# Four output accumulators per batch, a short lag between the two products, and the first batch's attention in quarters

## The chip, the cores and the metric

The kernel runs on one core of one Trainium2 chip. The metric is the device time of one execution in microseconds (us); less is better. TensorE is called PE below, VectorE DVE, ScalarE ACT, GpSimd POOL and SyncE SP. PE's results go to PSUM tiles; the kernel's two pools of them hold eight buffers of 128 x 512 fp32 between them.

## The reference

There are 8 batches and 8 heads, with x of 512 rows and state of 32 rows per head, 64 wide. State and x attend to one another, and the result, 8 x 544 rows of 512, goes through a two-layer network of width 2048.

```python
scores = scale * x @ state.T          # per batch and head, 512 x 32
xread = softmax(scores) @ state       # 512 x 64
scores2 = scale * state @ x.T         # 32 x 512
sread = softmax(scores2) @ x          # 32 x 64
y = concat([xread, sread], axis=2)    # 544 x 64, then heads side by side: 544 x 512
h = y @ w_in                          # 4352 x 2048
out = gelu_exact(h) @ w_out           # 4352 x 512, fp32
```

## The kernel before

**The work of a batch.** xread is never formed. `pmat` multiplies state by w_in into a tile P (256 x 2048 per batch, the two halves of the heads as two tiles of 128 rows), so that the first product is AT x P. `rearr` arranges x in the layout `x4`, `xtr` transposes it on PE into PSUM and DVE copies it out as `xT`; `scores` multiplies it by the block-diagonal state `sbd` into a PSUM tile pt, and ACT takes the exponential into `e`; `norm` (on DVE) sums over the 32 state rows, inverts and multiplies into `a`; `atr` transposes `a` to AT. `sread` (two halves, t = 0 and 1) multiplies `e` by `x4`, DVE scales the result into `srm`, and `srt` transposes that into XSR, where the state rows of all batches are collected.

**The two products.** `mm1(b, m)` makes chunk m (of 16) of the hidden layer for the 512 rows of batch b: two matmuls of 128 x 512 into a PSUM tile hp, then a gelu on ACT into `g`. `mm2` adds four chunks of `g` times w_out to one of four groups of 128 output rows: four matmuls into an accumulator `op`; four such quarters finish a group, DVE copies it to `osb`, and SP sends it out. `mm1_sr` and `mm2_sr` do the same for the 256 collected state rows at the end.

**The buffers.** `ps_f` has six buffers and holds everything short-lived: hp, the P tiles (two per 512 columns), transposes, pt, sread's and srt's results. `ps_o` has two, for the output accumulators. An accumulator's four quarters follow one another, so one or two groups are open at a time.

**The order.** It is written out by hand (`manual_schedule`): each engine runs its instructions in the order of the calls. A step is one `mm1` and, once 16 steps are done (`lag = 16`), one `mm2` call; the dictionaries `extra` (batches 0 and 1) and `steady` (the rest) put the attention of the next batch and the P groups between the steps. In `steady`, step 0 and 1 hold xtr, step 3 scores and norm, step 7 two P groups together, step 9 atr, steps 11 and 12 sread, step 13 two more P groups, step 14 srt. So a batch's output products run 16 steps behind its first products.

**The start.** The four quarters of batch 0's x (two heads each) are loaded as fp32, two by SP's queue and two by ACT's, and cast and arranged by DVE (`rearr0`); PE transposes them (`xtr0`), ACT copies all four out. `keep_warm` issues matmuls on a zero tile, 20 in all before the first product. All weights and the other batches' x are cast to bf16 by DMAs of the POOL queue, in the order w_in 0 and 1, the state, x1, w_in 2 and 3, w_out 0 and 1, x2, w_out 2 and 3, x3. At most eight of these transfers are under way: the ninth waits for the first to land.

The softmax here doesn't subtract the row's maximum and nothing guards it: scores larger than these inputs give would overflow.

## Time and profile before

| what | value |
| --- | --- |
| runs | 243.44, 243.13, 241.72 us (median 243.13) |
| the profiled execution, its own time | 240.81 us |
| its span in the profile | 238.6 us |
| granted TensorE clock, mean | 0.998 |
| PE busy | 223.9 us (94%) |
| ACT busy / DVE busy / POOL busy | 124.9 (52%) / 104.8 (44%) / 28.4 us (12%) |
| DMA busy share, first 48 us | about 0.8 to full, then about 0.1 to 0.4 |
| first mm1 starts | 14.73 us |
| first mm2 starts | 31.91 us |
| batch 2, 3 and 4 begin (first transposes in step 0) | 61.86, 86.73, 111.61 us |
| last matmul's copy begins / end of span | 234.85 / 238.6 us |

The profile is one execution, recorded by the hardware. The span is the time from the first to the last instruction in it; the execution's own time is 2.2 us longer. A line of a group or of the timeline names the source line, the engine, the operation, then the tile that is written and, after the arrow, the tiles that are read, with their shape; a bracket gives the time that the engine stood idle before and what ended it. Matmuls are pipelined: the recorded duration of one overlaps the next, so the work of PE is best read from start to start.

### The profile page before, as it was taken

How to read it: one execution, taken by the hardware profiler on the slowest of the kernel's cores; microseconds unless marked ns; L12 is line 12 of the kernel's file. 1: busy time of each engine (PE TensorE's matmuls, PEld its weight loads, DVE VectorE, ACT ScalarE, POOL GpSimd, SP SyncE). 2: the span in 40 equal slices, each digit the busy share in tenths (PEclk: the TensorE clock that was granted, in tenths of full speed). 3: DMA queues.
4: the chain of work that ended last, by engine and by line, in shares of the span. 5: the costliest groups of instructions: out<-in, count | busy, mean ns of one | idle time of the engine just before them, and what ended most of it. 6: DMA issues, size and time to landing. Idle time of an engine off the chain costs nothing.

```text
span 238.6 us, 3733 instructions
## 1 busy us (share of the span) xinstructions
PE 223.9 (94%) x1535; PEld 110.6 (46%) x1564; DVE 104.8 (44%) x198; ACT 124.9 (52%) x208; POOL 28.4 (12%) x41
## 2 busy tenths in 40 slices
PE   5996797989999999999999999999999999999993
PEld 1543243535544454444545454545454444557441
DVE  3646975574646433734283428343735112111120
ACT  2577742394486447745693559454945444335100
POOL 8745003103100400030002100000000000000000
PEclk9999999999999999999999999999999999999999
DMA  7999999720822180210111111111021111121022
GB/s 192 165 191 205 202 204 127 92 88 0 105 73 88 44 135 0 79 40 16 44 47 44 44 47 44 44 48 44 0 92 44 44 44 47 52 80 44 22 69 89
DMA packets 19889, 18.36 MB, mean 77 GB/s; under 512 B 3104, under 2 KB 15648, under 8 KB 19872
## 3 DMA queue, kind: packets, MB, share of 16 engines
q0 software_dynamic: 13376, 8.09, 24.7%
q1 hardware_dynamic: 5536, 9.31, 10.5%
q10 hardware_dynamic: 960, 0.72, 1.1%
q8 instruction: 12, 0.20, 0.3%
q14 instruction: 5, 0.04, 0.1%
HBM read 17.30 MB, written 8.91 MB: 110 GB/s over the span
## 4 chain that ended last, share of the span: by engine, by line
PE 89%; DVE 5%; DMA 2%; issue 1%; ACT 1%; ACTq 0%
PE op L364 46%; PE hp L330 22%; PE p_ps L306 4%; PE sr L264 3%; PE hps L378 3%; PE ops L390 3%; PE xT_ps L192 3%; DMA x0f<-in_x_dram 2%; PE warm_ps L121 2%; PE pt L200 2%; PE aT_ps L255 1%; DVE P L320 1%; DVE x L168 1%; DVE a L231 1%; DVE sbd L148 1%
## 5 line engine op out<-in xcount | busy, mean ns | idle before, releaser
L364 PE MATMUL op<-w_out_bf,g 128*128 128x512 bf16 x498 | 128.6, 379 | 1.0
L337 ACT ACTIVATE g<-hp 128x512 bf16<-128x512 f32 x128 | 73.9, 601 | 71.5 <-PE hp L330 67.7
L364 PEld LDWEIGHTS <-g 128*128 128x128 bf16 x512 | 50.0, 98 | 58.8
L330 PE MATMUL hp<-AT,P 128*128 128x512 bf16 x243 | 73.5, 380 | 2.7 <-DVE P L320 1.5
L350 DVE COPY osb<-op 128x512 f32<-128x512 f32 x31 | 21.4, 690 | 47.5 <-PE op L364 46.9
L330 PEld LDWEIGHTS <-P 128*128 128x128 bf16 x256 | 21.6, 97 | 24.9 <-issue 7.6
L320 DVE CAST P<-p_ps 128x512 bf16<-128x512 f32 x38 | 24.3, 684 | 8.1 <-PE p_ps L306 8.1
L168 POOL COPY x<-xb 128x1024 bf16<-128x1024 bf16 x10 | 10.4, 1042 | 96.1 <-PE sr L264 57.6
L228 DVE TENSOR_REDUCE cs<-e 128x16 f32<-128x512 bf16 x16 | 10.9, 682 | 22.9 <-ACT e L210 22.9
L318 ACT CAST P<-p_ps 128x512 bf16<-128x512 f32 x26 | 14.0, 590 | 7.1 <-PE p_ps L306 6.8
L193 DVE COPY xT<-xT_ps 128x1024 bf16<-128x1024 bf16 x14 | 9.6, 688 | 7.2 <-PE xT_ps L192 7.2
L306 PE MATMUL p_ps<-w_in_bf,sbd 64*32 64x512 bf16 x256 | 11.2, 383 | 0.5
L192 PE MATMUL xT_ps<-ident,x 128*128 128x128 bf16 x112 | 8.6, 220 | 3.0 <-DVE x L168 3.0
L231 DVE TENSOR_TENSOR a<-e,ics 128x512 bf16<-128x512 bf16 x16 | 11.1, 691 | 0.6
L210 ACT ACT_TABLE_LOAD x7 | 9.0, 1283 | 3.2 <-PE pt L200 3.2
L385 ACT ACTIVATE g_sr<-hps 128x256 bf16<-128x256 f32 x16 | 6.1, 383 | 8.4 <-PE hps L378 8.0
L192 PEld LDWEIGHTS <-x 128*128 128x128 bf16 x112 | 7.3, 98 | 6.7 <-DVE x L168 3.8
L337 ACT ACT_TABLE_LOAD x8 | 10.3, 1283 | 0.1
L264 PE MATMUL sr<-x,e 128*128 128x260 bf16 x64 | 10.0, 277 | 0.0
L273 DVE RECIPROCAL inv<-sr 128x1 f32<-128x1 f32 x16 | 2.6, 165 | 16.7 <-PE sr L264 16.6
L121 PE MATMUL warm_ps<-warm 128*128 128x512 bf16 x19 | 8.1, 564 | 1.2 <-DVE warm L74 1.2
L210 ACT ACTIVATE e<-pt 128x512 bf16<-128x512 f32 x16 | 8.8, 595 | 0.8 <-PE pt L200 0.7
(50 smaller groups left out, 117.3 us busy)
## 6 DMA issues: line engine op xcount, KB each, us to landing
out_dram<-osb SPq DMA_DIRECT2D x31, 256.0 KB, 2.3
xb<-in_x_dram POOLq DMA_DIRECT2D x7, 512.0 KB, 10.5
w_in_bf<-in_moe_w_in_dram POOLq DMA_DIRECT2D x8, 256.0 KB, 9.4
w_out_bf<-in_moe_w_out_dram POOLq DMA_DIRECT2D x4, 512.0 KB, 14.4
x0f<-in_x_dram SPq DMA_DIRECT2D x2, 256.0 KB, 3.3
x0f<-in_x_dram ACTq DMA_DIRECT2D x2, 256.0 KB, 4.8
out_dram<-osb SPq DMA_DIRECT2D x8, 64.0 KB, 1.7
st_bf<-in_state_dram POOLq DMA_DIRECT2D x1, 224.0 KB, 8.9
```

Of the source, the lines that this page charges most:

```text
L121: nc.tensor.matmul(ps, lhsT=warm[:, 0:128], rhs=warm, start=True, stop=True)
L192: nc.tensor.transpose(ps[:, ci, j, :], A.x4[:, j, 2 * half + ci, 2:130], ident)
L210: nc.scalar.activation(out=A.e[:, :, 64 * half:64 * half + 64], in_=A.pt.rearrange("p j t c n -> p (j t) (c n)"), func=AF.Exp, scale=scale,)
L231: nc.vector.tensor_tensor(out=A.a[:, :, hs].rearrange("p g (c n) -> p g c n", n=NS), in0=e4, in1=ics[:, :, :].to_broadcast((128, G, 2, NS) ...
L264: nc.tensor.matmul(sr, lhsT=A.e[:, 2 * j + t, :], rhs=A.x4[:, j, :, 1 + 65 * t:66 + 65 * t], start=(j == 0), stop=(j == SJ - 1),)
L306: nc.tensor.matmul(ps[t][32 * c:32 * c + 32, :], lhsT=sbd[64 * t:64 * t + 64, b, c, 32 * t:32 * t + 32], rhs=w_in_bf[64 * t:64 * t + 64, c ...
L318: nc.scalar.copy(out=dst, in_=ps[t])
L320: nc.vector.tensor_copy(out=dst, in_=ps[t])
L330: nc.tensor.matmul(hp, lhsT=Ps[b][:, t, m * 128:(m + 1) * 128], rhs=atts[b].AT[:, t, :], start=(t == 0), stop=(t == 1),)
L337: nc.scalar.activation(out=gs[b][:, m, :], in_=hp, func=AF.Gelu)
L350: nc.vector.tensor_copy(out=osb, in_=ps)
L364: nc.tensor.matmul(ps, lhsT=gs[b][:, m, j * 128:(j + 1) * 128], rhs=w_out_bf[:, m, :], start=(m == 0), stop=(m == MC - 1),)
```

## The change

It moves two of the eight PSUM buffers from the short-lived tiles to the accumulators (`ps_f` 6 to 4, `ps_o` 2 to 4). All four accumulators of a batch are open at once and are fed quarter by quarter: call (q, j) adds the chunks 4q to 4q + 3 to group j, in the order q, then j, five steps behind `mm1` (`lag = 5`). `pmat` does 512 columns per call, and the calls for one batch are spread over two batches' steps: f = 0 in step 13 of the batch before, f = 1, 2 and 3 in steps 1, 5 and 9 of its own. The next batch's xtr moves to steps 4 and 5, its scores and norm to step 8, sread to 10 and 11, srt to 12, atr to 14. `mm1_sr` moves into the steps of the last batch, `mm2_sr` takes its accumulators from `ps_f`.

Batch 0 and the first four steps of batch 1 are written out one by one. Batch 0's attention runs by quarters from copy to norm (`scores0`, `norm0`, PSUM from `ps_o`), the copies out of the transposes alternate between ACT and DVE, the last two quarters of its x are loaded as bf16 by the POOL queue, a gelu on a small tile (`gate`) stands ahead of the first real one, 11 warm-up matmuls stand before the first product, the memsets of POOL move to DVE, and each w_in chunk is followed by the w_out chunk of the same number in the POOL queue, with x2 and x3 last.

```diff
-    ps_f = ctx.enter_context(tc.tile_pool(name="ps_f", bufs=6, space=bass.MemoryType.PSUM))
-    ps_o = ctx.enter_context(tc.tile_pool(name="ps_o", bufs=2, space=bass.MemoryType.PSUM))
+    ps_f = ctx.enter_context(tc.tile_pool(name="ps_f", bufs=4, space=PSUM))
+    ps_o = ctx.enter_context(tc.tile_pool(name="ps_o", bufs=4, space=PSUM))
...
-    for c in range(HC):
-        eng = nc.sync if c % 2 == 0 else nc.scalar
-        eng.dma_start(out=x0f[:, :, c, :], in_=x0_rows[:, :, c, :])
+    for c in range(2):
+        nc.sync.dma_start(out=x0f[:, :, c, :], in_=x0_rows[:, :, c, :])
+    nc.vector.memset(warm, 0.0)
+    for c in range(2):
+        nc.gpsimd.dma_start(out=x0b[:, :, c, :], in_=x0_rows[:, :, 2 + c, :])
 
     make_identity(nc, ident)
-    nc.vector.memset(warm, 0.0)
-    nc.gpsimd.memset(sbd, 0.0)
+    nc.vector.memset(sbd, 0.0)
     for i in range(2):
-        nc.gpsimd.memset(x4s[i][:, :, :, 1:2], 1.0)
-        nc.gpsimd.memset(x4s[i][:, :, :, 130:131], 1.0)
+        nc.vector.memset(x4s[i][:, :, :, 1:2], 1.0)
+        nc.vector.memset(x4s[i][:, :, :, 130:131], 1.0)
...
-    load_w_in(0)
-    load_w_in(1)
+    for f in range(2):
+        load_w_in(f)
+        load_w_out(f)
     nc.gpsimd.dma_start(
         out=st_bf[:, 1:B, :, :].rearrange("q b t d -> q (b t) d"),
...
     load_x(1)
-    load_w_in(2)
-    load_w_in(3)
-    load_w_out(0)
-    load_w_out(1)
+    for f in range(2, FC):
+        load_w_in(f)
+        load_w_out(f)
     load_x(2)
-    load_w_out(2)
-    load_w_out(3)
     load_x(3)
...
+    def scores0(c):
+        A = atts[0]
+        A.pc = ps_o.tile([128, SJ, 2, NS], FP32, name="pc", tag="op")
+        for j in range(SJ):
+            nc.tensor.matmul(
+                A.pc[:, j, :, :], lhsT=A.xT[:, c, j, :], rhs=sbd[:, 0, c, :], start=True, stop=True
+            )
+        nc.scalar.activation(
+            out=A.e[:, :, NS * c:NS * c + NS],
+            in_=A.pc.rearrange("p j t n -> p (j t) n"),
+            func=AF.Exp,
+            scale=scale,
+        )
+
+    def norm0(c):
+        A = atts[0]
+        G = SJ * 2
+        e3 = A.e[:, :, NS * c:NS * c + NS]
...
-    def pmat(b, fs, act=()):
+    def pmat(b, f, act=()):
...
+        pool, tag = (ps_o, "op") if b == 0 and f == 0 else (ps_f, "f")
+        ps = [pool.tile([128, 512], FP32, name="p_ps", tag=tag) for t in range(2)]
...
-    def mm2(u):
-        b, r = u // 16, u % 16
-        if b == 0:
-            j, q = 2 * (r // 8) + r % 2, (r % 8) // 2
-        else:
-            j, q = r // 4, r % 4
+    def mm2(b, q, j):
         if q == 0:
-            ops[j % 2] = ps_o.tile([128, d_model], FP32, name="op", tag="op")
-        ps = ops[j % 2]
+            ops[b, j] = ps_o.tile([128, d_model], FP32, name="op", tag="op")
+        ps = ops[b, j]
...
     def mm2_sr(s):
-        ps = ps_o.tile([128, d_model], FP32, name="ops", tag="op")
+        ps = ps_f.tile([128, d_model], FP32, name="ops", tag="f")
...
+    rearr0(0)
+    rearr0(1)
     xtr0(0)
     xtr0(1)
+    rearr0(2)
+    rearr0(3)
+    scores0(0)
     xtr0(2)
+    scores0(1)
     xtr0(3)
+    norm0(0)
+    scores0(2)
+    norm0(1)
+    scores0(3)
+    nc.scalar.activation(out=gate, in_=hmask, func=AF.Gelu)
+    norm0(2)
+    norm0(3)
     keep_warm(2)
-    keep_warm(6)
-    pmat(0, (0,), act=((0, 0), (0, 1)))
-    keep_warm(4)
+    pmat(0, 0, act=(1,))
+    keep_warm(3)
     atr(0)
-    keep_warm(2)
+    M(0, 1, 2, 3)
+    U((0, 0), (0, 1))
+    pmat(0, 1)
+    U((0, 2))
+    M(4)
+    U((0, 3))
+    M(5)
+    sread(0, 0)
+    M(6)
+    sread(0, 1)
+    M(7)
+    srt(0)
+    U((1, 0))
+    state_prep(1, B)
+    begin(1)
+    rearr(1)
+    U((1, 1))
+    xtr(1, 0)
+    xtr(1, 1)
+    U((1, 2))
+    scores(1, 0)
+    scores(1, 1)
+    U((1, 3))
+    pmat(0, 2, act=(1,))
+    norm(1, 0)
+    norm(1, 1)
+    sread(1, 0)
+    M(8)
+    sread(1, 1)
+    M(9, 10)
+    srt(1)
+    M(11)
+    U((2, 0))
+    atr(1)
+    U((2, 1))
+    pmat(0, 3, act=(1,))
+    U((2, 2))
+    pmat(1, 0)
+    M(12)
+    U((2, 3))
+    M(13)
+    pmat(1, 1)
+    M(14, 15)
+    for j in range(SJ):
+        U((3, j))
+        M(16 + j)
+    begin(2)
+    rearr(2)
+    load_x(4)
+
+    lag = 5
+
+    def plan(b):
         nb = b + 1
         d = {}
+        if b > 1:
+            d[1] = [lambda: pmat(b, 1, act=(0, 1))]
+            if nb < B:
+                d[0] = [lambda: begin(nb), lambda: rearr(nb)]
+                if b + 3 < B:
+                    d[0].append(lambda: load_x(b + 3))
+        d[5] = [lambda: pmat(b, 2)]
+        d[9] = [lambda: pmat(b, 3)]
+        if nb < B:
+            d[4] = [lambda: xtr(nb, 0)]
+            d[5].append(lambda: xtr(nb, 1))
+            d[8] = [
+                lambda: scores(nb, 0),
+                lambda: scores(nb, 1),
+                lambda: norm(nb, 0),
+                lambda: norm(nb, 1),
+            ]
+            d[10] = [lambda: sread(nb, 0)]
+            d[11] = [lambda: sread(nb, 1)]
+            d[12] = [lambda: srt(nb)]
+            d[13] = [lambda: pmat(nb, 0)]
+            d[14] = [lambda: atr(nb)]
+        else:
+            for k in range(MC):
+                d.setdefault(k, []).append(lambda k=k: mm1_sr(k))
         return d
...
+    for b in range(1, B):
+        d = plan(b)
+        for k in range(4 if b == 1 else 0, MC):
+            for f in d.get(k, ()):
                 f()
+            mm1(b, k)
+            if 16 * b + k - lag >= 16:
+                Us(16 * b + k - lag)
+    Us(16 * B - 5)
     mm2_sr(0)
     mm2_sr(1)
+    for j in range(SJ):
+        Us(16 * B - 4 + j)
```

## The prediction

> **What bounds the kernel now.** First the page's head and its rows of slices: is there an engine that is never idle, and where is it not full?

> ```profile
> span 238.6 us, 3733 instructions
> ...
> PE 223.9 (94%) x1535; PEld 110.6 (46%) x1564; DVE 104.8 (44%) x198; ACT 124.9 (52%) x208; POOL 28.4 (12%) x41
> ...
> PE   5996797989999999999999999999999999999993
> ```

> TensorE (PE) is full from about 60 us to the end; the holes lie in the first ten slices of 5.97 us and in the last. The table by stretches (columns: stretch, its length, then busy time of PE, PEld, DVE, ACT, POOL) sizes them.

> ```profile
> 18.00:24.00 6.00, 3.83 (x47) 2.05 (x47) 3.79 (x7) 4.48 (x7) 3.13 (x4) 1.00 1.24 206
> 24.00:30.00 6.00, 4.75 (x43) 1.75 (x43) 5.86 (x12) 4.43 (x9) 0.00 (x0) 1.00 1.34 202
> 36.00:42.00 6.00, 4.44 (x30) 2.00 (x29) 3.38 (x8) 1.50 (x3) 2.19 (x3) 1.00 0.88 119
> 60.00:90.00 30.00, 29.84 (x217) 15.00 (x219) 15.28 (x28) 17.16 (x29) 3.50 (x4) 1.00 0.44 88
> ```

> So there are two regimes. Early, PE idles by turns (2.17, 1.25 and 1.56 us here); from 60 us it idles 0.16 us in 30, and whatever lengthens PE's queue there lengthens the kernel. Third, PE's timeline (start, duration, what; in brackets the wait before it):

> ```profile
> 36.46 0.41 PE L306 MATMUL p_ps<-w_in_bf,sbd 64*32 64x512 bf16 x8
> 36.80 0.39 PE L330 MATMUL hp<-AT,P 128*128 128x512 bf16 x1
> ...
> 50.31 0.62 PE L306 MATMUL p_ps<-w_in_bf,sbd 64*32 64x512 bf16 x16
> 51.97 0.38 PE L330 MATMUL hp<-AT,P 128*128 128x512 bf16 x1 [1.03 <-ACT g L337]
> 52.40 1.03 PE L364 MATMUL op<-w_out_bf,g 128*128 128x512 bf16 x4
> ```

> ```profile
> 62.31 0.60 PE L330 MATMUL hp<-AT,P 128*128 128x512 bf16 x2
> 62.74 1.03 PE L364 MATMUL op<-w_out_bf,g 128*128 128x512 bf16 x4
> 63.60 0.61 PE L192 MATMUL xT_ps<-ident,x 128*128 128x128 bf16 x8
> ...
> 66.64 0.63 PE L200 MATMUL pt<-sbd,xT 128*128 128x64 bf16 x16
> 67.11 0.38 PE L330 MATMUL hp<-AT,P 128*128 128x512 bf16 x1
> ...
> 72.38 0.63 PE L306 MATMUL p_ps<-w_in_bf,sbd 64*32 64x512 bf16 x16
> 72.94 0.60 PE L330 MATMUL hp<-AT,P 128*128 128x512 bf16 x2
> ```

> From start to start: an mm1 is 0.43 us, four mm2 matmuls 0.86, so a step is 1.29; a batch's scores 0.47. The row at 51.97 is the one that matters: after scores, the PSUM buffers were used up and PE stood 1.03 us for a gelu, with six buffers. Last, what ScalarE (ACT) does after scores that start at 66.64:

> ```profile
> 67.12 1.28 ACT L210 ACT_TABLE_LOAD   x1 [0.54 <-PE pt L200]
> 68.41 1.08 ACT L210 ACTIVATE e<-pt 128x512 bf16<-128x512 f32 x2
> 69.52 1.28 ACT L337 ACT_TABLE_LOAD   x1
> 70.81 2.06 ACT L337 ACTIVATE g<-hp 128x512 bf16<-128x512 f32 x4
> ```

> Counted from the scores' start, the two exps end at 2.37 and 2.86, and the gelu of the same step runs from 4.17 to 4.77. For those 4.8 us no hp buffer is given back. Six buffers covered that; the steady batches of before have no wait.

> **The change part by part.** M(m) is an mm1, U(q,j) four mm2 matmuls. Which buffer takes which bank, and what each instruction waits for, is fixed when the changed program is built, and I read it there.

> *Head.* Eleven warm-up matmuls instead of twenty; they cover waits and cost nothing by themselves. The chain starts with st_f as before (its cast at 3.93). rearr0 and the transposes of the first two quarters run as before, to 6.70. Then VectorE (DVE) has more in its queue: the xT copies of quarters 1 and 3 (0.43 each, the AT copy's row) and four norms in place of two. A half's norm is 1.62 (rows of 0.68, 0.25, 0.69); a quarter has half the elements, about 1.07. norm0(0) stands behind the last xT copy, which ends near 9.4, so the norms end at 9.4 + 4x1.07 = 13.7, against 12.50 before. But before, the a-transposes stood behind warm-ups until 13.83; now they run at 13.75. Then P's copy (0.65) and AT's on DVE, AT's other half on ACT: the first mm1 is done near 15.3, as before (14.73 and a wait for the second AT half). The gelu table load (1.28) now lies earlier, under the norms; before, it ended at 16.37. Head: 0. x0b by the POOL queue is not in the trace: bounded below by the x0f loads (3.3 us to landing, no delay), above by the first w_in load (6.2 us from issue: landed at 8.3, 0.9 late). I take no delay, since it is first in its queue. ident is moved behind these two issues (0.65 each), ready near 2.6 us: hidden under the wait for st_f; without that cover it would cost 1.3. The memsets moved to DVE (1.1 and four small) end before 3.2, hidden by the same wait. Bounds of the head: -1.2 (the norms no longer than their share of elements, 3.24 in all) to +1.5.

> *Queue order of the weights.* 1 MB read as fp32 takes 2.6 us in the POOL queue (issues freed by landings at 9.64, 10.91, 12.19, 13.59). From w_in 0 at 10.6 on, the new order gives w_out 0 at 13.2, w_in 1 15.8, w_out 1 18.4, x1 22, w_in 2 25, w_in 3 30, w_out 3 32.5, x2 35. Each is needed later than that (31, 40 and 45 us for the last weights): 0, and 2.6 late would still be hidden.

> *Batch 0 and the first four steps of batch 1.* The new U's fill PE, but DVE and ACT chains stand between them. Walking the written order with row durations, PE waits: U(0,0) for the fourth gelu 0.5; M(4) for the second P copy on DVE 0.45; srt(0) for its srm 0.55; xtr(1,0) for two sbd copies and rearr(1) 1.35 (before: 1.26 at the same place); M(8) 0.35 and M(10) 0.5 behind the table swap; srt(1) 2.2, since a P copy, two norms (3.24) and both srm pairs (0.7 each) must pass DVE while PE has 2.2 us of work; two U's for gelus 0.45; xtr(2,0) for an osb copy and rearr(2) 1.3. Sum 7.65. Before, from 14.73 to the start of batch 2 at 61.86, 47.1 us held 39.1 us of work by the same rows (32 mm1, 16 U, 11 P groups and the attention parts): 8.0 of waits. Gain 0.35; bounds -4 (half of my waits filled) to +2.

> *P in four single groups.* Rows: 36.37 to 36.80 is 0.43 for one group with its gap; 72.28 to 72.94 is 0.66 for two. Batches 2 to 7 go from 2x0.66 to 4x0.43: 0.40 each, 2.4 in all. This is PE work with no cover. Bounds 1.2 to 2.6.

> *Four buffers instead of six.* In step 8 (scores' start is 0) PE has: scores 0.47, M 0.90, U 1.76. pmat(b,3) starts at 1.85, but its second buffer was the first pt's: exp ends 2.37, so the group ends near 2.72. The next M needs the second pt's: 2.91 to 3.34; U to 4.20. sread needs M(8)'s buffer: gelu end 4.77, so 4.82 to 5.29. The next M needs M(9)'s: 5.33 to 5.76; U 6.62. Without waits this point is 5.24: 1.38 lost. Queued behind are all later matmuls of PE, which nothing gives back. In batch 2 alone the exp table load carries no wait and starts 0.63 earlier: 0.74 there. 5x1.38 + 0.74 = 7.6. The rest of the steady step finds its buffers free. Bounds: 4.4 (0.74 in all six) to 9 (1.5 each).

> [...] The row first: after the 1.03 us wait the mm1 at 51.97 and the U at 52.40 are 0.43 apart, the full rate, where the warm-ups of the first 10 us are 0.43 for one matmul. [...]

> *Tail.* Four accumulators now finish in the last four U's, 0.86 apart, so out transfers bunch up behind the eight small ones on the SP queue (0.47 per issue): +0.2, bounds 0 to 0.6. mm1_sr moves between the steps of the last batch: same matmuls, 0.

> **Sum:** 0 - 0.35 + 2.4 + 7.6 + 0.2 = +9.85 us. The profiled span of 238.6 becomes 248.4, its own time of 240.81 becomes 250.7. The runs shown have a median of 243.13, 2.3 above the profiled execution; against that I forecast 253.0.

> **The rivals.** (1) *The bank waits are hidden.* Place: step 8 of batches 1 to 6; price 7.6. It decides if the releases of sread and the next M come by 3.5 after the scores' start; then 243.1 + 2.25 = 245.4, within 1%: not slower. For: the library gives a tile the bank it expects free first, and six buffers had no wait in steady batches. Against: the gelu at 4.17 follows two table loads that no edit removes. (2) *The filling works.* The waits of batch 0 vanish, since DVE's chain is shorter than I walked: 253.0 - 7.65 = 245.4 too. For: two of every three early products are now work. Against: 2.2 of it is norms measured at 3.24. With half of the bank waits gone as well it would be 241.6, faster. (3) *The clock falls.* With nine warm-ups fewer, and stops in six batches, a step's matmuls after each stop take the warm-ups' 0.43: 1.29 lost six times, 7.7 more: 260.7. For: half rate did hold until about 12 us before. Against: the row at 51.97.

> **How the numbers follow.** Forecast 0.73, rival 1 0.11, rival 2 0.10, rival 3 0.06. The likeliest gives 253.0; its own terms at their lower ends, not all at once, reach 246 and at the upper 257.5. The range from 245.3 to 257.5 takes in the nearer halves of rivals 1 and 2 and leaves out their faster halves and rival 3, under 2 in 10. A measurement of this kernel can tell about 1% from no change, so 240.7 to 245.6 is "same": rivals 1 and 2 put 0.12 there and 0.07 below it, the rest is slower, 0.81.

> **What would show it.** In the changed profile: the first mm1 at 14.5 to 15.5; w_in and w_out never named as what ended a wait on PE; srT waiting some 2 us in batch 0; in steps 8 to 10 of batches 1 to 6 waits of PE on ACT's exp and gelu, a batch taking 24.87 + 0.4 + 1.38 = 26.65 us against 24.87; single P groups at 0.43. A steady batch of 25.3 us or less would make this wrong, and so would PE reaching step 4 of batch 1 before 46 us (I have 51).

## The result and the profile after

The changed kernel takes 251.66 us (median of four runs, 250.95 to 253.06); the kernel before, on the same chip, 242.43 us (240.27 to 243.44). The ratio is 1.04, with a 95% interval of 1.031 to 1.049. The profiled execution took 251.88 us, its span is 249.7 us against 238.6: 11.1 us more.

The page's head, PE's row and its slices, and the clock's row:

```profile
span 249.7 us, 3755 instructions
...
PE 230.6 (92%) x1555; PEld 109.7 (44%) x1555; DVE 112.7 (45%) x222; ACT 120.7 (48%) x198; POOL 28.0 (11%) x38
...
PE   5799759988999999999999899989999999999991
...
PEclk9679999999999999999999999999999999999997
```

The early holes are still there (the slices of 5, 7 and 8 tenths in the first ten), and slices of 8 tenths now stand among the later ones, where there were none. PE's busy time rose by 6.7 us, so part of the 11.1 is work or drawn-out work, and part is idle time in the steady batches. The table by stretches (stretch, length, busy PE, PEld, DVE, ACT, POOL, then clock, DMA share, GB/s) shows the second:

```profile
60.00:90.00 30.00, 29.01 (x200) 14.05 (x199) 16.63 (x32) 16.75 (x26) 4.08 (x4) 1.00 0.24 54
90.00:120.00 30.00, 29.29 (x207) 13.73 (x206) 14.28 (x29) 15.27 (x24) 4.01 (x4) 1.00 0.24 54
```

PE idles 0.99 and 0.71 us in 30, where it was 0.16 and 0.35 before. The list of PE's waits (who waited for what; total us, times, longest) names the place:

```profile
PE sr L293 <- ACT g L363: 2.7, 6, 0.5
PE srT L316 <- DVE srm L303: 2.3, 2, 2.0
PE xT_ps L228 <- DVE x L170: 2.3, 2, 1.3
...
PE p_ps L334 <- ACT e L244: 0.9, 5, 0.2
PE p_ps L334 <- DMA w_in_bf<-in_moe_w_in_dram: 0.8, 2, 0.7
```

The first and the fourth come once a batch: sread (L293) waits for a gelu and the P group (L334) for an exponential, to get their PSUM buffers. PE's timeline of that step, in the first such batch, shows that these rows understate it:

```profile
56.84 0.63 PE L237 MATMUL pt<-sbd,xT 128*128 128x64 bf16 x16
...
58.70 0.39 PE L334 MATMUL p_ps<-w_in_bf,sbd 64*32 64x512 bf16 x1
59.26 0.41 PE L334 MATMUL p_ps<-w_in_bf,sbd 64*32 64x512 bf16 x7 [0.17 <-ACT e L244]
59.74 0.59 PE L356 MATMUL hp<-AT,P 128*128 128x512 bf16 x2
60.17 1.02 PE L386 MATMUL op<-w_out_bf,g 128*128 128x512 bf16 x4
61.65 0.62 PE L293 MATMUL sr<-x,e 128*128 128x260 bf16 x4 [0.45 <-ACT g L363]
```

The P group's first matmul starts at 58.70, the other seven at 59.26: 0.56 from start to start for one of eight matmuls that take 0.43 together elsewhere, with a bracket of only 0.17, since the 0.39 recorded for the first one covers the rest. From 60.17 to 61.65 four matmuls that need 0.86 take 1.48. ACT's timeline of the same moments:

```profile
57.31 1.28 ACT L244 ACT_TABLE_LOAD   x1 [0.54 <-PE pt L237]
58.61 1.08 ACT L244 ACTIVATE e<-pt 128x512 bf16<-128x512 f32 x2
59.71 1.28 ACT L363 ACT_TABLE_LOAD   x1
61.00 1.08 ACT L363 ACTIVATE g<-hp 128x512 bf16<-128x512 f32 x2
```

The first exponential ends near 59.15, the first gelu near 61.60, and PE goes on 0.1 and 0.05 us later. So PE is paced here by ACT's chain of table load, two exponentials, table load and gelu. Counted from the scores' start, sread begins 4.81 us later; the prediction's walk had 4.82. A batch (first transpose of step 4 to the next) takes 26.67 us from 103.13 to 129.80, and again to 156.47 and 183.14; before it took 24.87.

Step 4 of batch 1 starts at 51.11, where the prediction has 51; the kernel before has no such point to set beside it, since its order is another. The last difference is the tail, the stretch from the last matmul to the end of the span. DVE's timeline, the last copy:

```profile
245.06 0.42 DVE L371 COPY osb<-op 128x256 f32<-128x256 f32 x1 [0.58 <-DMA out_dram<-osb]
```

The last matmul ends at 244.62 and the span at 249.7, 5.1 us later; before it was 234.82 and 238.6, 3.8 us. Up to the last matmul the change costs 9.8 us, behind it 1.3.

### The profile page after: what moved, and what is told of

Same layout as the page of the kernel before. It is cut to its first block, busy times and chain, and to the rows that moved or that the text cites. A ratio compares the mean times of both kernels' runs of the same rounds, so it can differ in the third digit from the quotient of the medians.

```text
span 249.7 us, 3755 instructions
## 1 busy us (share of the span) xinstructions
PE 230.6 (92%) x1555; PEld 109.7 (44%) x1555; DVE 112.7 (45%) x222; ACT 120.7 (48%) x198; POOL 28.0 (11%) x38
## 4 chain that ended last, share of the span: by engine, by line
PE 75%; ACT 12%; DVE 5%; DMA 4%; issue 1%; POOL 1%; SPq 0%; ACTq 0%; DVEq 0%; POOLq 0%
PE op L386 37%; PE hp L356 19%; PE p_ps L334 4%; ACT L363 3%; ACT L244 3%; PE sr L293 3%; ACT g L363 3%; PE hps L400 3%; PE xT_ps L228 3%; DMA w_in_bf<-in_moe_w_in_dram 3%; PE ops L412 3%; ACT e L244 3%; PE aT_ps L284 1%; DVE P L346 1%; DMA out_dram<-osb 1%
## 5 line engine op out<-in xcount | busy, mean ns | idle before, releaser
L386 PE MATMUL op<-w_out_bf,g 128*128 128x512 bf16 x512 | 131.2, 379 | 0.2
L356 PE MATMUL hp<-AT,P 128*128 128x512 bf16 x256 | 76.2, 380 | 1.4 <-DVE P L346 0.5
L346 DVE CAST P<-p_ps 128x512 bf16<-128x512 f32 x49 | 31.6, 684 | 22.9 <-PE p_ps L334 22.8
L170 POOL COPY x<-xb 128x1024 bf16<-128x1024 bf16 x10 | 10.6, 1062 | 102.3 <-PE sr L293 68.6
L257 DVE TENSOR_REDUCE cs<-e 128x16 f32<-128x512 bf16 x14 | 9.5, 681 | 26.7 <-ACT e L244 26.7
L334 PE MATMUL p_ps<-w_in_bf,sbd 64*32 64x512 bf16 x256 | 15.9, 393 | 1.7 <-ACT e L244 0.9
L293 PE MATMUL sr<-x,e 128*128 128x260 bf16 x64 | 10.0, 277 | 2.7 <-ACT g L363 2.7
L334 PEld LDWEIGHTS <-sbd 64*32 64x32 bf16 x256 | 4.1, 89 | 17.8 <-issue 15.5
L344 ACT CAST P<-p_ps 128x512 bf16<-128x512 f32 x15 | 8.2, 588 | 7.4 <-PE p_ps L334 7.4
L407 ACT ACTIVATE g_sr<-hps 128x256 bf16<-128x256 f32 x16 | 6.2, 384 | 11.1 <-PE hps L400 11.1
L228 PE MATMUL xT_ps<-ident,x 128*128 128x128 bf16 x112 | 8.5, 220 | 2.3 <-DVE x L170 2.3
L260 DVE TENSOR_TENSOR a<-e,ics 128x512 bf16<-128x512 bf16 x14 | 9.7, 692 | 0.5
L293 PEld LDWEIGHTS <-e 128*128 128x128 bf16 x64 | 6.1, 96 | 8.1 <-issue 4.4
L400 PE MATMUL hps<-XSR,w_in_bf 128*128 128x256 bf16 x64 | 9.6, 273 | 0.0
## 6 DMA issues: line engine op xcount, KB each, us to landing
xb<-in_x_dram POOLq DMA_DIRECT2D x7, 512.0 KB, 13.2
w_out_bf<-in_moe_w_out_dram POOLq DMA_DIRECT2D x4, 512.0 KB, 13.2
```

Source lines behind the costliest of these rows:

```text
L170: eng.tensor_copy(out=A.x4[:, :, :, 2 + 64 * t:66 + 64 * t].rearrange("p j c d -> p c j d"), in_=xbs[b][:, 4 * t:4 * t + 4, :].rearrange(" ...
L228: nc.tensor.transpose(ps[:, ci, j, :], A.x4[:, j, 2 * half + ci, 2:130], ident)
L260: nc.vector.tensor_tensor(out=A.a[:, :, hs].rearrange("p g (c n) -> p g c n", n=NS), in0=e4, in1=ics[:, :, :].to_broadcast((128, G, 2, NS) ...
L293: nc.tensor.matmul(sr, lhsT=A.e[:, 2 * j + t, :], rhs=A.x4[:, j, :, 1 + 65 * t:66 + 65 * t], start=(j == 0), stop=(j == SJ - 1),)
L334: nc.tensor.matmul(ps[t][32 * c:32 * c + 32, :], lhsT=sbd[64 * t:64 * t + 64, b, c, 32 * t:32 * t + 32], rhs=w_in_bf[64 * t:64 * t + 64, c ...
L346: nc.vector.tensor_copy(out=dst, in_=ps[t])
```

## The experiments

Each run is compared with the kernel before on its own chip, in three groups (medians of the kernel before 240.53, 239.97 and 240.03 us). Periods are read from step to step in PE's timeline.

**Single P groups, in the kernel before.** The edit reaches the P groups of batches 3 to 7.

```diff
-        d[7] = [lambda: pmat(nb, (0, 1), act=((0, 1), (1, 1)))]
+        d[6] = [lambda: pmat(nb, (0,), act=((0, 1),))]
+        d[7] = [lambda: pmat(nb, (1,), act=((1, 1),))]
...
-        d[13] = [lambda: pmat(nb, (2, 3), act=((2, 1), (3, 1)))]
+        d[13] = [lambda: pmat(nb, (2,), act=((2, 1),))]
         d[14] = [lambda: srt(nb)]
+        d[15] = [lambda: pmat(nb, (3,), act=((3, 1),))]
```

> The kernel before, with one edit: the P groups of batches 3 to 7 stand one by one (steps 6, 7, 13 and 15) instead of two together (steps 7 and 13); six buffers stay. Theory: a single group costs 0.43 us of PE, a pair 0.66, so a steady batch goes from 24.87 to 25.27 us and the kernel by 5 x 0.40 = +2.0 us (about 244.4 against 242.4). Rival (the split is free, PE's gaps around a group are only modelled): 24.87 and no change.

Measured: 242.71 us (242.42 to 243.37), ratio 1.0094 (1.0066 to 1.0122). PE's timeline, the starts of two batches:

```profile
86.56 0.61 PE L192 MATMUL xT_ps<-ident,x 128*128 128x128 bf16 x8
...
111.89 0.61 PE L192 MATMUL xT_ps<-ident,x 128*128 128x128 bf16 x8
```

A batch takes 25.33 us, 0.46 more than with pairs, and the time rises by 2.2, against 5 x 0.46 = 2.3. It is work on PE, and nothing covers it.

**Four short-lived buffers, in the kernel before.** Nothing else is changed; the accumulators stay at two.

```diff
-    ps_f = ctx.enter_context(tc.tile_pool(name="ps_f", bufs=6, space=bass.MemoryType.PSUM))
+    ps_f = ctx.enter_context(tc.tile_pool(name="ps_f", bufs=4, space=bass.MemoryType.PSUM))
```

> The kernel before, with one edit: ps_f has four buffers instead of six; order and accumulators are as before, two buffers' room is unused. Theory (a P pair takes all four buffers, so the next mm1 waits for the first copy out of PSUM): 0.6 us after each pair, 1.2 per steady batch (period about 26.1 against 24.87), with batches 0 and 1 some +1 to +2: +8 to +9 us, about 251. Rival (four are enough for the old order, and only the new order's place of scores and sread makes waits): +0 to +2 us.

Measured: 248.84 us (248.64 to 250.06), ratio 1.0359 (1.0315 to 1.0403): 8.3 us more. PE's waits in it:

```profile
PE hp L330 <- ACT P L318: 3.8, 10, 0.5
...
PE p_ps L306 <- ACT g L337: 1.4, 2, 1.3
```

The size is near that of the changed kernel, but the place is another one: here a pair of P groups takes all four buffers at once, and the next mm1 waits for ACT's copy of one of them. That four are too few is shown in both orders; where they are missed depends on the order.

**The buffers' users spread, in the changed kernel.** Four buffers stay, but no P group and no sread stand in the two steps behind the scores.

```diff
-        d[9] = [lambda: pmat(b, 3)]
+        d[7] = [lambda: pmat(b, 3)]
...
-            d[10] = [lambda: sread(nb, 0)]
-            d[11] = [lambda: sread(nb, 1)]
-            d[12] = [lambda: srt(nb)]
+            d[11] = [lambda: sread(nb, 0)]
+            d[12] = [lambda: sread(nb, 1)]
             d[13] = [lambda: pmat(nb, 0)]
-            d[14] = [lambda: atr(nb)]
+            d[14] = [lambda: srt(nb), lambda: atr(nb)]
```

> The changed kernel, with the users of buffers moved away from behind the scores: the P group f = 3 in step 7 instead of 9, sread in steps 11 and 12 instead of 10 and 11, srt in 14 instead of 12. Nothing else. Theory (the buffers are held from the scores to the gelu of step 8): no wait of PE in steps 8 to 12, a steady batch 25.27 instead of 26.67 us, in all -7.6 us, about 244. Rival (the short lag of five steps leaves mm2 waiting for gelus whatever the order): period stays near 26.7, about 251.5.

Measured: 244.11 us (243.86 to 246.86), ratio 1.0176 (1.0125 to 1.0226). The last matmul ends at 236.96, 7.66 earlier than in the changed kernel. Its table by stretches and its timeline behind the scores:

```profile
60.00:90.00 30.00, 30.00 (x207) 14.69 (x206) 17.01 (x34) 17.65 (x28) 5.22 (x5) 1.00 0.24 53
```

```profile
57.13 0.63 PE L237 MATMUL pt<-sbd,xT 128*128 128x64 bf16 x16
57.60 0.60 PE L356 MATMUL hp<-AT,P 128*128 128x512 bf16 x2
58.03 1.03 PE L386 MATMUL op<-w_out_bf,g 128*128 128x512 bf16 x4
58.89 0.59 PE L356 MATMUL hp<-AT,P 128*128 128x512 bf16 x2
```

PE is never idle, and a batch takes 25.33 us, as with single groups and six buffers. So the stop is one of order as much as of number. By the order of the calls the scores take two of the four buffers, the next two mm1 the other two, and the third mm1 finds one that the exponential has emptied; without a P group and an sread among them, nobody comes too early.

**The exponential's table earlier, in the changed kernel.** A small Exp on `gate` behind the gelu of step 7 lets the load run before the scores are done; what it writes is used by nothing.

```diff
             mm1(b, k)
+            if k == 7 and b + 1 < B:
+                nc.scalar.activation(out=gate, in_=hmask, func=AF.Exp)
```

> The changed kernel, with one more small Exp (128 x 4, into gate) behind the gelu of step 7 in batches 1 to 6, so that the exp table is loaded while PE is still in steps 7 and 8. Theory (the chain is table load, two exps, table load, gelu): the exps start 0.4 us earlier in five batches, 0.2 later in batch 2; PE's waits per batch fall from 1.40 to about 1.0, so -1.8 us, about 249.9. Rival (the waits are for VectorE, behind its norms): no change.

Measured: 250.94 us (249.63 to 252.01), ratio 1.0431 (1.0397 to 1.0466). ACT's timeline, the second batch:

```profile
110.58 1.28 ACT L552 ACT_TABLE_LOAD   x1
111.88 0.20 ACT L552 ACTIVATE gate<-hmask 128x4 f32<-128x4 f32 x1
111.99 1.07 ACT L244 ACTIVATE e<-pt 128x512 bf16<-128x512 f32 x2
113.07 1.28 ACT L363 ACT_TABLE_LOAD   x1
114.37 1.08 ACT L363 ACTIVATE g<-hp 128x512 bf16<-128x512 f32 x2
```

The scores start at 110.63, so the gelu starts 3.74 later instead of 4.16. The batch takes 26.24 us (77.87 to 104.11), 0.43 less. So PE follows ACT's chain one to one. The profiled total shows less of it, because the clock fell once in batch 0 there (0.50 from 36.8 to 40.2): step 4 of batch 1 starts at 52.42, where the run with the users spread has 50.95, 1.47 us that are no part of the edit (the last section shows such a fall).

**The tail: three groups behind the state read's output.** One of the last four U's is moved ahead of `mm2_sr`.

```diff
     Us(16 * B - 5)
+    Us(16 * B - 4)
     mm2_sr(0)
     mm2_sr(1)
-    for j in range(SJ):
+    for j in range(1, SJ):
         Us(16 * B - 4 + j)
```

> The changed kernel, with the first of the last four accumulators finished before the two mm2_sr instead of after them. Theory: the last copy waited 0.58 us for an osb buffer whose transfer was late, behind eight small and three large transfers bunched on SP's queue; with one group less in the bunch the wait is gone and the stretch from the last matmul to the end falls from 5.2 us to about 4.2 (before: 3.8): -1.0, about 250.7. Rival (the end is one transfer's landing, whatever is ahead of it): 5.2 stays.

Measured: 253.74 us (251.44 to 254.51), ratio 1.057 (1.0526 to 1.0613). DVE's last copy:

```profile
244.37 0.42 DVE L371 COPY osb<-op 128x256 f32<-128x256 f32 x1 [0.17 <-PE op L386]
```

The wait for the DMA is gone, and the time is not: 249.7 - 244.34 = 5.4 us from the last matmul to the end. So the wait named in the changed kernel's tail was not its cause. What is, the run with the state read early tells.

**Batch 0 in another order, in the changed kernel.** `state_prep` and `rearr(1)` go earlier in DVE's queue, the norms of batch 1 go behind both of its sread, `rearr(2)` goes ahead of the last U's; some U's move with them.

```diff
     U((0, 3))
+    state_prep(1, B)
     M(5)
     sread(0, 0)
     M(6)
     sread(0, 1)
+    begin(1)
+    rearr(1)
     M(7)
-    srt(0)
     U((1, 0))
-    state_prep(1, B)
-    begin(1)
-    rearr(1)
-    U((1, 1))
+    srt(0)
...
-    norm(1, 0)
-    norm(1, 1)
     sread(1, 0)
     M(8)
     sread(1, 1)
+    norm(1, 0)
+    norm(1, 1)
...
```

> The changed kernel, with VectorE's order in the hand-written stretch changed: state_prep and rearr(1) earlier, the two norms of batch 1 behind its sread, U(1,3) behind the P group, rearr(2) ahead of the four U(3,j). Theory (these waits are chains on VectorE, which nothing else holds): the waits of 1.27 (xtr), 1.98 (srT), 0.35 (srT) and 1.02 us (xtr) fall to about 0.6 together, step 4 of batch 1 starts near 47 us instead of 51.1, -4.0 in all, about 247.7. Rival (the weights' transfers end these waits): no change.

Measured: 247.47 us (247.3 to 248.41), ratio 1.0306 (1.027 to 1.0342). Step 4 of batch 1 starts at 46.77, against 51.11. PE's waits:

```profile
PE sr L293 <- ACT g L363: 2.7, 6, 0.5
PE aT_ps L284 <- DVE a L260: 1.4, 1, 1.4
```

The waits of srT and of the transposes L228 are gone; the norms, now later, hold the a-transposes 1.4 us instead. So 4.3 us of batch 0 were the order of DVE's queue.

**All three edits together.**

> The changed kernel with the three reorderings together: users of buffers moved away from the scores, the tail, and VectorE's order in the first stretch. If the terms add: 251.7 - 7.65 - 1.0 - 4.0 = 239.0 on the scale where before is 242.4, a ratio of 0.986 to the kernel before, so faster than both. If the waits only move from one place to the next: not below 243.

Measured: 240.28 us (239.71 to 241.93), ratio 1.0014 (0.999 to 1.0037). The span is 239.4. The changed kernel's whole loss is taken back, but the gain over the kernel before that the terms' sum gave (a ratio of 0.986) did not come: the tail is still 5.3 us, and the first products ran near half rate (their first eight matmuls took 3.18 us from start to start against 1.87 in the run before; step 4 of batch 1 at 48.11 against 46.77).

**Five warm-ups fewer, in the changed kernel.**

```diff
-    keep_warm(2)
     pmat(0, 0, act=(1,))
-    keep_warm(3)
     atr(0)
```

> The changed kernel without the five warm-up matmuls around the first P group. Theory of the prediction (warm-ups only fill waits): first mm1 up to 0.4 us earlier, the transposes of a no longer standing behind three half-rate matmuls, and the total within 0.5 of 251.7. Rival (they bring TensorE to full rate): the half rate, which lasted to 15 us, lasts until 18 or longer, and up to 1.7 us are lost, about 253.4.

Measured: 254.62 us (253.92 to 255.33), ratio 1.0596 (1.0558 to 1.0634); step 4 of batch 1 starts at 54.66. The a-transposes wait 1.93 us for the norms with an idle PE, and the first eight matmuls of the products then take 3.52 us from start to start, near half rate, against 2.18 in the changed kernel's first profile. At the first srT the run is 2.03 us late. The other 1.5 of its 3.55 us come from a fall of the clock behind the second srT (0.50 from 40.03 on), which the changed kernel also shows without this edit, so the warm-ups have no proven part in it. And the start at half rate appears with all warm-ups too, in the run with all three edits and in the changed kernel's second profile: how often the five prevent it, one profile can't say. All four runs (253.92 and more) lie above the changed kernel's first four (253.06 and less), though two of its later ones reach 254.2. So that the warm-ups only fill waits, as the prediction took them, is unlikely, and what each is worth stays open.

**The state read's products early in the last batch.** In the changed kernel, so that the eight 64 KB rows of `mm2_sr` leave the end.

```diff
-                d.setdefault(k, []).append(lambda k=k: mm1_sr(k))
+                d.setdefault(k // 2 + 3, []).append(lambda k=k: mm1_sr(k))
+            d[12] = [lambda: mm2_sr(0)]
+            d[14] = [lambda: mm2_sr(1)]
...
-    Us(16 * B - 5)
-    mm2_sr(0)
-    mm2_sr(1)
-    for j in range(SJ):
-        Us(16 * B - 4 + j)
+    for j in range(5):
+        Us(16 * B - 5 + j)
```

> The changed kernel with the state read's projection out of the end: its sixteen first products go two to a step into steps 3 to 10 of the last batch, its two second products into steps 12 and 14, and only five groups of the four accumulators follow the last first product. The matrix products are the same in number, so the last matmul should end where it did (near 244.3). Theory, the small transfers: the eight 64 KB rows of the state read take 8 x 0.42 = 3.4 us of SP's issue queue and stand ahead of the last big rows; gone, the stretch from the last matmul to the end falls from 5.2 us to about 3.8 to 4.2, the span to 248.3 to 248.7, ratio to the kernel before about 0.005 lower than the changed kernel's. Rival, the big rows: four accumulators finish within 2.6 us whatever stands ahead, and four 256 KB rows keep the DMA engines full at some 370 GB/s: the stretch stays at 5 us or more and the span at 249.3 to 249.7.

Measured: 251.83 us (250.46 to 253.21), ratio 1.0485 (1.0422 to 1.0547), against 1.0516 (1.0452 to 1.0581) of the changed kernel in the same group: no difference that these runs can tell, because both scatter by 3 us. The profile tells more. The rows of DMA busy tenths in the last 8.6, 8.7 and 7.9 us of the span, cut in 40 slices, of the kernel before, the changed one and this one:

```profile
DMA  7281730000000199900000000000297950010000
```

```profile
DMA  1000000191926656399999999999980000000000
```

```profile
DMA  0000000000005998299948999999600000000100
```

Before, the engines idle between the groups' transfers and the last one finds them free. In the changed kernel they are full for 2.6 us without a break behind the small rows. Here the small rows are gone, gaps appear, and the stretch from the last matmul (244.42) to the end (248.9) is 4.5 us.

The rows split the tail in two. The last busy slice ends near 237.1, 247.5 and 246.7: 2.3, 2.9 and 2.3 us behind the last matmul. So without the small rows the transfers end as soon behind the last matmul as before, though four accumulators still finish within 2.6 us. The small rows account for this part, 0.6 us. The rest lies behind the last transfer: to the end of the span it is 1.5 us before and 2.2 in the two others, with no output left to move (a single 1 there is one packet of an instruction queue). The two runs above in the kernel before's order have 1.5 there, and every run in the changed order has 2.1 to 2.2. These 0.7 us came with the changed program whatever its tail held; no run shows what they are.

**All three, with that tail in place of the other.**

> The kernel with spread users and the new order of batch 0 (span 239.4 with the earlier tail), now with the state read's projection early in the last batch. Terms add: 244.47 - 7.65 - 4.35 = 232.5 for the last matmul at a full clock, up to 1.5 later if the first products run at half rate as they did there. Theory of the small transfers: 3.8 to 4.2 behind it, span 236.3 to 238.2, ratio 0.985 to 0.995. Rival of the big rows: 5.2 behind it, span 237.7 to 239.2, ratio 0.992 to 1.001.

Measured: 240.51 us (238.54 to 241.51), ratio 1.0003 (0.9973 to 1.0032); the profiled execution has 237.4 us of span, step 4 of batch 1 at 46.75, the last matmul at 232.93 and a tail of 4.5. Span and last matmul are where the theory's terms put them; the tail lies between the two theories, and the ratio of all runs above the theory's range. Its runs scatter by 3 us, and their median is not the profiled one.

**The same with two more warm-ups.**

```diff
-    keep_warm(2)
+    keep_warm(4)
     pmat(0, 0, act=(1,))
     keep_warm(3)
```

> The kernel of the run before with four warm-up matmuls instead of two ahead of the first P group. Theory, the clock at the first products is a matter of how closely work stands in the last microseconds before them: the first eight matmuls run in about 2.0 us instead of 2.9 to 3.3, and it is 0.5 to 1.3 us faster than the run before. Rival: the stop for the norms of batch 0, not the warm-ups ahead of the P group, decides (13.08 to 13.45), or it differs from run to run: no difference, or 0.4 slower for two half-rate warm-ups ahead of the P group's eight matmuls.

Measured: 239.54 us (238.85 to 239.84), ratio 0.9964 (0.9946 to 0.9983). The profiled spans of the two kernels are equal (237.4), and both show the first products at the full rate (eight matmuls in 1.87 us from start to start; step 4 of batch 1 at 46.75). What differs is the scatter: the highest run falls from 241.51 to 239.84, while the lowest goes from 238.54 to 238.85. The two warm-ups may make the full-rate start the usual one: the kernel with all three edits, whose instructions are the same up to the first products as those of the run before, had started at near half rate. That is an inference from the scatter of eight and ten runs; no two traces show it side by side. It is the one version here whose interval lies below the kernel before, by 0.4%, which is less than the 1% that the prediction took for the least difference a measurement of this kernel can tell.

**The changed kernel once more.**

> The changed kernel itself, once more, beside the others on the same chip. If the tail's spread and the stops are what the first profile shows, ratio 1.04 (1.031 to 1.049) and a span near 249.7; the theory that a 1.98 us stop in batch 0 drops the clock in some executions and not in others leaves room for 1.5 us more.

Measured: 251.39, 251.63, 254.15 and 254.24 us (median 252.89), ratio 1.0516 (1.0452 to 1.0581). The profile is of the longest, span 252.1, and it can be laid on the first one, since the instructions are the same. PE's timeline of the first profile, then of this one:

```profile
14.23 2.34 PE L356 MATMUL hp<-AT,P 128*128 128x512 bf16 x8
16.41 2.28 PE L386 MATMUL op<-w_out_bf,g 128*128 128x512 bf16 x8
...
36.75 0.27 PE L316 MATMUL srT<-istack,srm 128*128 128x32 bf16 x4 [1.98 <-DVE srm L303]
36.86 0.59 PE L356 MATMUL hp<-AT,P 128*128 128x512 bf16 x2
37.29 1.24 PE L386 MATMUL op<-w_out_bf,g 128*128 128x512 bf16 x4
```

```profile
14.64 3.17 PE L356 MATMUL hp<-AT,P 128*128 128x512 bf16 x8
17.65 2.16 PE L386 MATMUL op<-w_out_bf,g 128*128 128x512 bf16 x8
...
37.87 0.29 PE L316 MATMUL srT<-istack,srm 128*128 128x32 bf16 x4 [1.99 <-DVE srm L303]
38.00 1.01 PE L356 MATMUL hp<-AT,P 128*128 128x512 bf16 x2
38.81 1.91 PE L386 MATMUL op<-w_out_bf,g 128*128 128x512 bf16 x4
```

At srT this one is 1.12 us late: the products start 0.41 later, the first eight matmuls take 3.01 us from start to start against 2.18, and the next eight win 0.12 back. Behind the same stop of 1.99 us the matmuls then take about double (1.01 us recorded for an mm1 against 0.59, at a granted clock of 0.50), and step 4 of batch 1 starts at 53.50, 2.39 late. From there to the end it is 198.6 us in both. So the scatter of the changed kernel's times, at least between these two executions, is TensorE's clock in the first 41 us, at two places; the first of them shows in the matmuls' times only, the second in the granted clock too.

## Why the prediction was right

| term | predicted, us | measured, us | from |
| --- | --- | --- | --- |
| start, to the first mm1 | 0 | -0.5 and -0.1 | 14.23 and 14.64 against 14.73 |
| start and batch 0 together | -0.35 | -0.6 | users spread: 236.96 - 234.82, less 6 x 0.46 |
| batch 0 to step 4 of batch 1 | at 51 | 51.11; 53.50 where the clock fell | two profiles |
| P in single groups | +2.4 for six batches | +2.8; in the run with five, +2.2 | 6 x 0.46; 242.71 - 240.53 |
| four buffers | +7.6 | +7.5 | 244.62 - 236.96, less 0.16 by which the users spread run starts step 4 of batch 1 earlier |
| a steady batch | 26.65 | 26.67 | three batches |
| up to the last matmul | +9.65 | +9.8 | 244.62 - 234.82 |
| tail | +0.2 | +1.3 | 5.1 against 3.8 |

The mechanism was the one forecast, in its place and size: five full stops of 1.34 (26.67 - 25.33; 1.38 was forecast) and a smaller one of 0.81 in batch 2, where the exponential's table is loaded without a wait (76.99 to 103.13 is 26.14; 0.74 was forecast). The chain behind it (scores, table load, exponential, table load, gelu, release) could be walked from rows of the kernel before, because none of its durations changed. Shortening the chain by 0.42 shortened the batch by 0.43, which is the strongest evidence that it sets PE's pace.

The walk through batch 0 held item by item too. From start to start in the first profile, less the work by the same rows, its nine waits come to 0.48, 0.39, 0.52, 1.44, 0.42, 0.49, 2.15, 0.49 and 1.19 us, 7.57 in all, in the order in which the prediction lists them with 7.65. So 51 for step 4 of batch 1 was not luck.

The mis-sized term is the tail, 1.3 where 0.2 was taken and 0.6 was the upper bound. The prediction counted SP's issues and left out that the DMA engines would be full. One 256 KB row every 0.86 us asks for 305 GB/s, and with the small rows still in the queue the engines, full, moved some 370; so the transfers end 0.6 us later behind the last matmul. The other 0.7, between the last transfer and the end of the span, the prediction had no term for, and their cause stays open.

The step from the span to the median was wrong as well. The 2.3 us between the profiled execution and the median of the first three runs of before was added to the changed kernel too; its median is 0.2 below its profiled execution, and a fourth run of the kernel before, 240.27, took that one's median to 242.43. That 253.0 lies so close to 251.66 is luck in part: a tail taken 1.1 us too small and a step to the median 2.5 us too large (2.3 + 0.2). The difference of the two kernels, +9.85 in the forecast, is 9.2 by the medians of the first runs, 11.1 by the two spans, and 12.9 by the medians of the last group (252.89 - 240.03).

Smaller points went otherwise. w_in was named as what ended two waits of PE, 0.8 us in all, at the first P group, against the sign that the prediction gave; in the first profile this held three warm-ups and the a-transposes behind them some 0.5 us beyond the norms' end (12.60 against 13.08), in the second it did not appear. The norms ended at 12.60 there, not 13.7, mostly because the transposes before them ran near the full rate (eight in 0.73 us, against 1.03 in the run with all three edits, where the a-transposes wait for the norms until 13.45). ident was ready at 3.4, not 2.6, so its move was not wholly hidden: st_f's cast starts at 4.11, not 3.93. And the waits of batch 0 were not fixed by DVE's work, as the walk took them: 4.3 us of them could be filled by order alone.

Of the rivals, the first (bank waits hidden) is out by PE's named waits; the second (batch 0 filled) was out for this order, and another order reached 4.3 of its 7.65 us. The third, the falling clock, did come, but not in its place. The stops of the steady batches cost no clock at all: the granted clock is 1.00 in every stretch from 60 to 210 us in both profiles, and the mm1 and the U behind the stop at 59.26 start 0.43 us apart, the full rate. The loss came in the first 41 us, in some executions, for 1.1 and 1.3 us.

The same stop of 1.98 us was followed by half rate in some executions only, and in which ones went with where it lay among the clock's switches (last section). What stays open is the 0.7 us behind the last transfer, and whether the two further warm-ups act by way of the clock.

## What to carry to other kernels

When a PSUM pool is cut, find the longest time in which the engine that empties it gives nothing back (here ACT's two table loads and two exponentials, 4.8 us), count what the issuing engine wants to open in that time, and move those users elsewhere: this kernel lost 7.5 us to a P group and an sread that stood a step or two from where there was room. Accumulators fed in parallel also finish in parallel (here four within 2.6 us), so the last transfers bunch up; put small outputs well ahead of the end, and judge the tail by the DMA engines' busy row and not by the wait that is named. Where waits can't be removed, warm-up matmuls that fill them are not to be counted as free to drop: with five fewer, the first srT came 0.9 and 2.0 us later here than in the changed kernel's two profiles.

## What the runs showed of the hardware

A stop of 1.98 to 1.99 us on PE was followed by half rate in three profiles (early exponential table, fewer warm-ups, the changed kernel's second) and not in four others with the same stop (the changed kernel's first, users spread, the tail, the state read early). Where the stop lies among the switches of the granted clock separates them. In the changed kernel's first profile the clock falls at 8.19, rises at 15.02 and falls at 247.13, behind the last matmul: 2 and 70 times 3.413 us from the first switch. In its second it falls at 37.60 and rises at 41.01, 3.41 us later. In the six other profiles that show a fall and a rise (single P groups, four buffers, early exponential table, the tail, fewer warm-ups, the state read early) the two are 3.4 or 6.8 us apart. So a profile can be cut into windows of 3.413 us counted from a switch (in the users spread run, which has none but a fall behind its last matmul, from that one), which lie differently in each, and the table by stretches can be taken along them. First the second profile, then the first one:

```profile
34.19:37.60 3.41, 1.36 (x7) 0.42 (x5) 3.23 (x9) 2.12 (x4) 0.00 (x0) 1.00 1.46 197
37.60:41.01 3.41, 3.14 (x15) 1.45 (x16) 0.51 (x2) 0.60 (x1) 2.52 (x3) 0.50 0.67 90
```

```profile
32.09:35.50 3.41, 2.10 (x11) 0.88 (x10) 3.27 (x8) 3.09 (x5) 0.00 (x0) 1.00 1.45 199
35.50:38.91 3.41, 2.12 (x19) 1.16 (x20) 1.41 (x5) 0.60 (x1) 0.05 (x1) 1.00 1.45 197
```

In the second profile PE is idle for 2.05 us of one window, and the granted clock (the column ahead of the DMA share) is 0.50 in the whole next one. In the first profile a boundary cuts the same stop in two: 1.31 and 1.29 us idle, and the clock stays. The idlest window around that stop, in the seven profiles that have it:

| profile | idlest window, us | PE idle in it, us | clock in the next window |
| --- | --- | --- | --- |
| early exponential table | 33.37 to 36.79 | 2.32 | 0.50 |
| changed, second | 34.19 to 37.60 | 2.05 | 0.50 |
| five warm-ups fewer | 36.62 to 40.03 | 1.98 | 0.50 |
| tail | 34.90 to 38.31 | 1.60 | 1.00 |
| users spread | 32.29 to 35.71 | 1.43 | 1.00 |
| changed, first | 32.09 to 35.50 | 1.31 | 1.00 |
| state read early | 31.69 to 35.10 | 1.31 | 1.00 |

The stops of 0.45 to 0.6 us in each steady batch leave no window from 60 to 225 us with more than 0.71 us idle in the changed kernel's first profile, and in neither of its two profiles does the clock fall there.

The recorded clock does not show all of it: in the second profile it is 1.00 from 14 to 18 us, while eight matmuls take 3.01 us from start to start there and 1.87 in the run with all three edits and the early state read. At 0.43 and 0.22 us a matmul, an estimate from the 3.01 us puts the rise to the full rate near 17.2 us; counted back from the fall at 37.60, a window's boundary lies at 17.12. Whether these boundaries decide how the first products start as well was not shown, nor whether the two more warm-ups have a part in it.
